# A fused attention and two-MLP kernel: the second product of the first MLP through DRAM by a seven-product scheme, the attention on fixed half steps

## The chip, the cores and the metric

The kernel runs on one core of one Trainium2 chip. The metric is the device time of one execution in microseconds (us), the median over several executions; lower is better.

## What is computed

Three pieces follow each other, all in float32, on 8 batches of 576 tokens (4608 tokens in all, 512 features, 2048 hidden features):

```python
a = softmax(phi, axis=2)                     # (8, 8, 576, 32), exp after subtracting the maximum, sum + 1e-9
k_m = einsum('bhsm,bhsd->bhmd', a, k)        # memory of 32 rows per head
v_m = einsum('bhsm,bhsd->bhmd', a, v)
attn = softmax(q @ k_m.T / sqrt(64))
x = heads_to_features(attn @ v_m)            # (4608, 512)
x = (s * relu(x @ w_in1) ** 2 + b) @ w_out1  # first MLP, 512 -> 2048 -> 512
out = (relu(x @ w_in2) ** 2) @ w_out2        # second MLP, the same sizes
```

The weights arrive as 64-bit floats and are narrowed on the chip.

## The kernel before

All large matmuls take float32 operands as two rounded halves (fp32r), a high part (a cast on ScalarE) and a remainder (a subtraction on VectorE), and add three products of them; `split3` names the three. A matmul here is 128x128 weights against 256, 288 or 384 columns.

**Attention and first MLP, interleaved.** `attention(b)` (L219) is a generator that issues the attention of one batch in pieces: the softmax of phi, the memory products `kvs` (L272), their transposes (L317, L318), the transposes of q (L340), the scores (L355), their softmax, and the transposed probabilities `pt`, split in two (L392, L393). The values are not multiplied with the probabilities: `v_fold` (L469) multiplies them into w_in1 first (`vps`, L459) and splits the result in `vp`, so that the first product of the MLP, `h1` (L480), is `vp` times `pt`: six matmuls of 288 columns (half a batch) for each of the 16 blocks of 128 hidden features (L490). Its result is rectified, squared and split on ScalarE and VectorE (L496 to L499) into `g`, and `x1` (L502) at once multiplies `g` with the stored split w_out1: twelve matmuls of 288 columns (L507), accumulated over the 16 blocks in four PSUM banks. The sums leave through `x1_store` (L513) into DRAM (`x1d`). There are 256 such steps (8 batches, 2 halves, 16 blocks), in the order of the list `steps`, `h1` two steps ahead of `x1`. Between the matmul groups `slot()` counts places and `advance()` lets the attention of a later batch go on for a piece when its due place is reached; what a piece asks for in `yield` is how many places it wants to pass.

**Weights of the second MLP.** From step 66 on, `narrow` and `combine` (L109, L142) prepare the seven combinations of both weight matrices of the second MLP that a seven-product scheme (Strassen's, in Winograd's form) needs, and store them in DRAM (`wcd`, `wod`): 16 units, narrowed, summed and split on ScalarE and VectorE beside the steps.

**Second MLP.** It goes in two phases, each by the seven-product scheme. The first product (L803) goes over 6 pairs of 384-token halves; for each of eight units of hidden features and each of the seven products there are six matmuls of 384 columns. `sums` and `split_x` make the seven combinations of the input, `chain` adds the seven results into four quadrants, which are rectified, squared and stored in DRAM (`gd`). The second product (L868) reads them back in 18 blocks of 256 tokens, makes the seven combinations of each and runs 24 matmuls of 256 columns for each.

Pools: PSUM has 4 banks for `acc`, 2 for `hps` and 2 for everything else in the interleaved part, 8 free banks later. All loads and nearly all stores are issued by the SP queue, in program order. A scheduler orders each engine's instructions from the program; each engine then works through its own list in order.

## Time and profile before

| | |
|---|---|
| runs of the kernel (us) | 1501.75, 1505.45, 1505.59; median 1505.45 |
| the profiled execution | 1501.85 us, of which 1500.0 us from the first to the last instruction |
| TensorE (PE) busy | 1462.7 us (98%), weight loads (PEld) 1408.7 us |
| VectorE (DVE) busy | 930.8 us (62%) |
| ScalarE (ACT) busy | 800.0 us (53%) |
| GpSimd (POOL) busy | 1.0 us |
| DMA | 235.8 MB, 157 GB/s on the mean |
| mean granted TensorE clock | 0.994 of 2.4 GHz |

How to read it: an engine's busy time is the time in which at least one of its instructions was in work. TensorE's matmuls overlap each other, so that the mean duration of one is no measure of how many fit into a microsecond; the starts of equal groups are. The stages by TensorE: until 31.5 us the first batch's attention, until 777.6 us attention and first MLP interleaved, from 779.4 us the first product of the second MLP, from about 1134 us its second product. What lies outside of the span is 1.85 us in the profiled execution.

### The profile page before, as it was taken

Reading aid. Unit: us, or ns where it says so; the run is one execution under the profiler, and the core shown is the slowest. Engines: PE = TensorE matmul, PEld = TensorE weight load, DVE = VectorE, ACT = ScalarE, POOL = GpSimd, SP = SyncE. Lnnn points to the kernel's source line nnn. Section 1 sums busy time; section 2 is a strip of 40 time slices with the busy share of each in tenths; the row PEclk is TensorE's granted clock in tenths of the full one; section 3 lists DMA queues with packets and bytes.
Section 4 is the critical chain, followed back from the end, with each engine's and each line's share of the span. In section 5 each row is a group of like instructions: output and inputs, shape, how many; then the busy total and the mean of one; then the engine's idle time right before and its main releaser. Section 6 shows DMA issues by size and latency. Waiting matters only on the chain.

```text
span 1500.0 us, 29921 instructions
## 1 busy us (share of the span) xinstructions
PE 1462.7 (98%) x12400; PEld 1408.7 (94%) x12400; DVE 930.8 (62%) x1528; ACT 800.0 (53%) x1637; POOL 1.0 (0%) x7
## 2 busy tenths in 40 slices
PE   5899999999999999999999999999999999999998
PEld 4789989989989899998999999999999999999998
DVE  6985464866758667544234655656556776667774
ACT  4677565776757767656542543434344444444442
POOL 0000000000000000000000000000000000000000
PEclk8999999999999999999999999999999999999999
DMA  9763323537365363403218524435498444443431
GB/s 306 232 195 129 125 80 96 168 128 238 122 240 175 132 230 129 164 28 134 81 50 346 169 97 157 151 103 183 162 331 321 141 138 132 139 132 122 138 116 29
DMA packets 157559, 235.77 MB, mean 157 GB/s; under 512 B 44912, under 2 KB 130928, under 8 KB 148848
## 3 DMA queue, kind: packets, MB, share of 16 engines
q1 hardware_dynamic: 157264, 233.60, 46.7%
q8 instruction: 97, 1.59, 0.4%
q14 instruction: 38, 0.31, 0.1%
q10 hardware_dynamic: 160, 0.26, 0.0%
HBM read 145.49 MB, written 88.34 MB: 156 GB/s over the span
## 4 chain that ended last, share of the span: by engine, by line
PE 88%; DVE 5%; DMA 5%; ACT 2%; issue 1%; SPq 0%; ACTq 0%; DVEq 0%
PE acc L507 24%; PE qa L868 13%; PE pa L803 13%; PE hps L490 12%; PE qc L868 7%; PE pc L803 6%; PE qb L868 3%; PE pb L803 3%; PE vps L459 2%; DMA kv<-in_v_dram 2%; DMA gd<-gr 1%; PE sp L355 1%; PE qps L340 1%; PE kvs L272 1%; DMA wt<-in_moe_w_in_dram 1%
## 5 line engine op out<-in xcount | busy, mean ns | idle before, releaser
L507 PE MATMUL acc<-g,wo 128*128 128x288 f32 (+1 forms) x3072 | 468.5, 299 | 0.4 <-DVE wo L138 0.3
L507 PEld LDWEIGHTS acc<-g,wo 128*128 128x128 f32 x3072 | 425.0, 189 | 23.2 <-ACT r L497 11.7
L490 PE MATMUL hps<-pt,vp 128*128 128x288 f32 x1536 | 257.2, 301 | 1.7 <-DVE pt L393 0.9
L499 DVE TENSOR_TENSOR g<-r,g 128x288 fp32r<-128x288 f32 x256 | 116.4, 456 | 196.3 <-ACT g L498 193.8
L490 PEld LDWEIGHTS hps<-pt,vp 128*128 128x128 f32 x1536 | 220.9, 190 | 12.5 <-issue 7.5
L868 PE MATMUL qa<-w,gc 128*128 128x256 f32 x1728 | 216.2, 283 | 1.3 <-ACT o L731 1.1
L803 PE MATMUL pa<-xc,w 128*128 128x384 f32 x1152 | 213.4, 337 | 1.5 <-issue 1.4
L868 PEld LDWEIGHTS qa<-w,gc 128*128 128x128 f32 x1728 | 210.7, 191 | 1.7 <-ACT o L731 1.3
L803 PEld LDWEIGHTS pa<-xc,w 128*128 128x128 f32 x1152 | 202.1, 188 | 2.1 <-issue 1.6
L496 ACT ACTIVATE r<-hps 128x288 f32<-128x288 f32 x256 | 105.1, 411 | 164.9 <-PE hps L490 162.0
L756 DVE TENSOR_TENSOR gc<-h,gc 128x1024 fp32r<-128x1024 f32 x102 | 124.6, 1223 | 92.8 <-ACT gc L755 92.8
L755 ACT CAST gc<-h 128x1024 fp32r<-128x1024 f32 x102 | 107.4, 1053 | 54.7 <-PE qb L868 27.2
L497 ACT ACTIVATE r<-r 128x288 f32<-128x288 f32 x256 | 113.6, 445 | 6.4
L498 ACT CAST g<-r 128x288 fp32r<-128x288 f32 x256 | 110.5, 432 | 6.2
L868 PE MATMUL qc<-w,gc 128*128 128x256 f32 x864 | 109.3, 283 | 0.4 <-ACT gc L755 0.4
L803 PE MATMUL pc<-xc,w 128*128 128x384 f32 x576 | 108.5, 337 | 0.0
L868 PEld LDWEIGHTS qc<-w,gc 128*128 128x128 f32 x864 | 105.9, 191 | 0.7 <-ACT gc L755 0.7
L803 PEld LDWEIGHTS pc<-xc,w 128*128 128x128 f32 x576 | 101.2, 188 | 0.0
L811 DVE SCALAR_TENSOR_TENSOR gr<-gr 128x384 f32<-128x384 f32 x144 | 79.5, 557 | 3.7
L720 DVE TENSOR_TENSOR gr<-pa,gr 128x384 f32<-128x384 f32 x48 | 26.5, 554 | 66.7 <-PE pa L803 66.7
L720 DVE TENSOR_TENSOR gr<-pb,gr 128x384 f32<-128x384 f32 x48 | 26.6, 554 | 66.4 <-PE pb L803 43.3
L808 ACT ACTIVATE gr<-pa 128x384 f32<-128x384 f32 x48 | 23.6, 491 | 72.1 <-PE pa L803 72.0
(261 smaller groups left out, 1440.0 us busy)
## 6 DMA issues: line engine op xcount, KB each, us to landing
gd<-gr SPq DMA_DIRECT2D x96, 384.0 KB, 3.5
h<-gd SPq DMA_DIRECT2D x34, 1024.0 KB, 4.8
wt<-in_moe_w_out_dram SPq DMA_DIRECT2D x16, 1024.0 KB, 5.3
q<-in_q_dram SPq DMA_DIRECT2D x72, 128.0 KB, 3.1
x1d<-xo SPq DMA_DIRECT2D x16, 576.0 KB, 3.6
out_dram<-o SPq DMA_DIRECT2D x70, 128.0 KB, 2.3
kv<-in_k_dram SPq DMA_DIRECT2D x23, 384.0 KB, 5.0
kv<-in_v_dram SPq DMA_DIRECT2D x23, 384.0 KB, 6.4
```

What stands on the lines that cost most here:

```text
L490: nc.tensor.matmul(hps[:, :NB1], lhsT=w[:, wi], rhs=pt[xi][:, hp, t0:t0 + NB1], start=(i == 0), stop=(i == 5))
L496: nc.scalar.activation(r[:, :NB1], hps[:, :NB1], AF.Relu)
L497: nc.scalar.activation(r[:, :NB1], r[:, :NB1], AF.Square)
L498: st["act"] = nc.scalar.copy(g[0][:, :NB1], r[:, :NB1])
L499: st["dve"] = nc.vector.tensor_tensor(out=g[1][:, :NB1], in0=r[:, :NB1], in1=g[0][:, :NB1], op=ALU.subtract)
L507: nc.tensor.matmul(acc[d][:, :n], lhsT=wo1[:, f, wi, d * P:d * P + P], rhs=g[xi][:, :n], start=(first and i == 0), stop=(store is not None ...
L720: nc.vector.tensor_tensor(out=out, in0=bank, in1=other, op=ALU.add)
L755: nc.scalar.copy(c[:, :, 0, :], of)
L756: nc.vector.tensor_tensor(out=c[:, :, 1, :], in0=of, in1=c[:, :, 0, :], op=ALU.subtract)
L803: nc.tensor.matmul(to, lhsT=w[:, wi, k], rhs=xc[e][:, xi, k], start=(start and n == 0), stop=(n == 5), skip_group_check=True)
L811: nc.vector.scalar_tensor_tensor(out=done, in0=done, scalar=0.0, in1=done, op0=ALU.max, op1=ALU.mult)
L868: nc.tensor.matmul(to, lhsT=casts[n, e][:, u, xi], rhs=w[:, wi].rearrange("p k c -> p (k c)"), start=(start and u == 0 and i == 0), stop=( ...
```

## The change

The first MLP is taken apart in two phases like the second.

**Phase one, attention and first product.** The list of steps, `x1` and the paced generators are gone. There are 256 half steps (`slot`), each one call of `hidden`: the same six matmuls as in `h1`, then only the rectification, on ScalarE, into a tile `r` (128 x 576). Each pair of half steps stores `r` to DRAM (`rd`). The pieces of the attention of later batches are laid over the half steps by a table, `on(slot, piece)`: in each batch of 32 half steps the scores, memory products and folds of a later batch stand at places 8, 16 and 24, the q transposes at 4, 13 and 21, and so on. All of batch 1's softmax of phi and memory products stand ahead of the first half step. PSUM has 3 banks for `hps`, 2 for `kvs` and 3 for everything else. In the second to fourth batch `wo1_narrow` narrows w_out1, and GpSimd adds up its rows (`wacc`, eight operations of 128x1024) for the bias term; in the last two batches `wo1_combos` makes the seven combinations of w_out1 in SBUF.

**Phase two, second product by seven products.** Nine blocks of 512 tokens. `quad` loads the four quarters (128 x 2048 each) of a block from `rd`; ScalarE squares them, `sums` makes seven combinations in place, and each is cast and split in two halves (128 x 1024); 48 matmuls of 256 columns for each of the seven products. The combinations are asked for three half products ahead (`ready1.upto`); the pool `c` has five buffers for them. The results leave with scale and bias to `x1d`.

**Weights of the second MLP.** `combine` for w_in2 runs in phase two of the first MLP (one piece at each half product), for w_out2 in the first product of the second MLP. `chain` and `sums` take the seven products in another order everywhere, and `sums` needs no extra tile; the second MLP's loops are the same otherwise. All of its first weights are loaded at the end of phase two, into the tiles that w_out1's combinations held.

```diff
     ND = DM // P
     NV = DFF // 512
-    NB1 = S // 2
+    HB = S // 2
+    NU = NF // 2
     TP = 384
     NPAIR = NT // (2 * TP)
...
-    SEGS += [(b, half, 0, NF) for b in range(2, B) for half in range(2)]
-    SLOTS = 6
+    TB = 512
+    NBLK1 = NT // TB
+    NBLK2 = NT // 256
+    XG = 1536
+    SB = 2 * NF
...
+    rd = [[dram.tile([P, NU, S], F32, name=f"rd{b}_{h}") for h in range(2)] for b in range(B)]
...
+    def fold(b, n):
+        w = c_p.tile([P, 2, 2, 512], F32R, tag="c", name="vp")
+        ts = [bank("vps") for _ in range(2)]
...
+            nc.scalar.copy(w[:, hp, 0, :], t)
+            nc.vector.tensor_tensor(out=w[:, hp, 1, :], in0=t, in1=w[:, hp, 0, :], op=ALU.subtract)
+        at["vp", b, n] = w
...
+    def hidden(b, f, half, r):
+        pt = at["pt", b]
         hps = ps_h.tile([P, 512], F32, tag="h", name="hps")
...
+        t0 = half * HB
...
-            w = folded[b, f // 4][:, hp, :, (f % 4) * P:(f % 4) * P + P]
-            for wi, xi in ((0, 0), (0, 1), (1, 0)):
-                nc.tensor.matmul(hps[:, :NB1], lhsT=w[:, wi], rhs=pt[xi][:, hp, t0:t0 + NB1],
+            w = at["vp", b, f // 4][:, hp, :, (f % 4) * P:(f % 4) * P + P]
+            for wi, xi in split3:
+                nc.tensor.matmul(hps[:, :HB], lhsT=w[:, wi], rhs=pt[xi][:, hp, t0:t0 + HB],
                                  start=(i == 0), stop=(i == 5))
                 i += 1
-            slot()
-        r = tmp.tile([P, NB1], F32, tag="r", name="r")
-        g = g1[at % 3]
-        nc.scalar.activation(r[:, :NB1], hps[:, :NB1], AF.Relu)
-        nc.scalar.activation(r[:, :NB1], r[:, :NB1], AF.Square)
-        st["act"] = nc.scalar.copy(g[0][:, :NB1], r[:, :NB1])
-        st["dve"] = nc.vector.tensor_tensor(out=g[1][:, :NB1], in0=r[:, :NB1], in1=g[0][:, :NB1], op=ALU.subtract)
-        return g
-
-    def x1(acc, b, half, f, g, first, store):
-
-        n = NB1 + 2 if (b, half) == (0, 0) else NB1
+        nc.scalar.activation(r[:, t0:t0 + HB], hps[:, :HB], AF.Relu)
+
...
+    def wo1_narrow(u):
+
+
...
+            two = rc_p.tile([P, 2, 2, 512], F32, tag="rc", name="wo1")
+            wo1[u], wo1[u + 1] = two[:, 0], two[:, 1]
+        yield from narrow(t, wo1[u])
+        yield
+        if u == 0:
+            nc.gpsimd.tensor_copy(wacc, wo1[u])
+        else:
+            nc.gpsimd.tensor_tensor(out=wacc, in0=wacc, in1=wo1[u], op=ALU.add)
+
...
-    def x1_store(acc, b, half, part, last, keep):
-
-
-        t0 = b * S + half * NB1
...
-            if not last:
-                if part is None:
-                    nc.scalar.copy(o[:, d], src)
-            elif d % 2:
-                nc.vector.tensor_scalar(out=o[:, d], in0=src, scalar1=s_sb[:, 0:1], scalar2=wsum[:, d:d + 1],
-                                        op0=ALU.mult, op1=ALU.add)
-            else:
-                nc.scalar.activation(o[:, d], src, AF.Identity, scale=s_sb[:, 0:1], bias=wsum[:, d:d + 1])
-            if d == ND - 1 and not keep:
-                nc.sync.dma_start(x1d[t0 // XG][:, :, t0 % XG:t0 % XG + NB1] if last else partd[b][half], o)
-        store.o = o
-        return store
-
...
+    def wo1_combos(u):
+        tiles = unit_tiles(u)
+        for i, t in enumerate(tiles):
+            w2["one", u, i] = t.bitcast(F32R)
+        yield from combos(of_out(wo1.pop(u)), lambda: w2["one", u, 0], lambda: w2["one", u, 1])
...
+    def quad(n, h, j):
+        t = rc_p.tile([P, NU, 256], F32, tag="rc", name=f"r{h}{j}")
+        t0, t1 = n * TB + j * 256, n * TB + j * 256 + 256
         a = t0
...
+            m = min(t1 - a, S - a % S)
+            nc.sync.dma_start(t[:, :, a - t0:a - t0 + m], rd[a // S][h][:, :, a % S:a % S + m])
+            a += m
+        return t
...
+    def block_ready(n):
+        def cast(e, of):
+            for uh in range(2):
+                c = c_p.tile([P, NU // 2, 2, 256], F32R, tag="c", name="rcast")
+                src = of[:, uh * NU // 2:(uh + 1) * NU // 2]
+                nc.scalar.copy(c[:, :, 0, :], src)
+                nc.vector.tensor_tensor(out=c[:, :, 1, :], in0=src, in1=c[:, :, 0, :], op=ALU.subtract)
+                cast1[n, e, uh] = c
+        b11, b12, b22, b21 = quads.pop(n)
+        return sums(b11, b12, b21, b22, cast, lambda t: nc.scalar.activation(t, t, AF.Square))
...
+    front(0)
+    w1_narrow(0)
+    for g in range(NJG):
+        kvs(0, g)
+    kv_norm(0)
+    front(1)
+    kv_turn(0)
...
+    events = {}
+
+    def on(slot, go, *args):
+        events.setdefault(slot, []).append(lambda: go(*args))
+
+    for n in range(1, NV):
+        on((6, 14, 22)[n - 1], fold, 0, n)
+    for i in range(4, 2 * NV):
+        on((8, 10, 16, 18)[i - 4], w1_narrow, i)
+    for b in range(1, B):
+        z = SB * (b - 1)
+        for g, a in enumerate((8, 16, 24)):
+            on(z + a, scores, b, g)
...
+            y = SB * (b - 2) + (8 if b == 2 else 0)
+            for g, a in enumerate((8, 16, 24)):
+                on(y + a, kvs, b, g)
+            on(y + 26, kv_norm, b)
...
+        for n in range(NV):
+            on(z + 8 * n + 8, fold, b, n)
+        for g, a in enumerate((4, 13, 21)):
+            on(z + a, q_turn, b, g)
+        for g, a in enumerate((9, 17, 25)):
+            on(z + a, q_exp, b, g)
+            on(z + a + 1, q_sum, b, g)
+        for g, a in enumerate((13, 21, 29)):
+            on(z + a, p_turn, b, g)
+    on(SB * 5 + 21, wo1_sum)
+
...
+    for slot in range(SB * B):
...
+        if half == 0:
+            r = r_p.tile([P, S], F32, tag="r", name="r")
+        hidden(b, f, half, r)
+        if half == 1:
+            nc.sync.dma_start(rd[b][f // NU][:, f % NU], r)
...
+    def chain(e, banks, n, run, name):
+
+
+        key = "acacaba"[e]
+        start = e in (0, 1, 5)
+        if start:
+            banks[key] = bank(name + key)
+        to = banks[key][:, :n]
+        run(to, start)
+        return to
...
-    def advance():
-
-        task, pace = tasks[0]
...
-    def slot():
-        work["at"] += 1
-        if tasks and work["at"] >= work["due"]:
-            advance()
...
+    for n in range(NBLK1):
+        banks, outs = {}, {}
+        if n == NBLK1 - 1:
+            for _ in win:
+                pass
+            w64x.close()
...
+        for e in range(7):
+
+            def run(to, start):
+                for uh in range(2):
+                    half = 14 * n + 2 * e + uh + 3
+                    ready1.upto(half // 14, half % 14 // 2)
+                    next(win, None)
+                    for d in range(2):
+                        for u in range(NU // 2):
+                            w = weight("one", uh * NU // 2 + u, e)
+                            for i, (wi, xi) in enumerate(split3):
+                                nc.tensor.matmul(
+                                    to[:, d * 256:d * 256 + 256], lhsT=w[:, wi, d], rhs=cast1[n, e, uh][:, u, xi],
+                                    start=(start and uh == 0 and d == 0 and u == 0 and i == 0),
+                                    stop=(uh == 1 and u == NU // 2 - 1 and i == 2), skip_group_check=True)
+            to = chain(e, banks, 512, run, "y")
+            which, high = ((0, 0), (1, 1), (0, 1), (0, 1), (1, 1), (0, 0), (1, 0))[e]
+            key = which, high
+            if key not in outs:
+                outs[key] = o1_p.tile([P, 2, 256], F32, tag="o", name="yo")
+                for d in range(2):
+                    nc.scalar.activation(outs[key][:, d], to[:, d * 256:d * 256 + 256], AF.Identity,
+                                         scale=s_sb[:, 0:1], bias=wsum[:, 2 * which + d:2 * which + d + 1])
+            else:
+                o = outs[key].rearrange("p d t -> p (d t)")
+                nc.vector.scalar_tensor_tensor(out=o, in0=to, scalar=s_sb[:, 0:1], in1=o, op0=ALU.mult, op1=ALU.add)
+            if e > 2:
+                t0 = n * TB + high * 256
+                nc.sync.dma_start(x1d[t0 // XG][:, 2 * which:2 * which + 2, t0 % XG:t0 % XG + 256], outs[key])
+            if e == 4 and n + 1 < NBLK1:
+                quads[n + 1] = [quad(n + 1, *hj) for hj in QUADS]
```

What this does to the order of the engines' lists shows at three places.

VectorE ahead of the first half step. Before, from the first batch's row sums to the first split probabilities (`rs` are the row sums, `kb` the turned keys, `m_` and `l_` maxima and sums of the scores, `vp` the folded weights, `pt` the probabilities):

```order
L303 RECIPROCAL rs<-rs 128x2
L130 TENSOR_SCALAR wx<-wx 128x1024
L131 SCALAR_TENSOR_TENSOR wx<-wt,wx 128x1024
L324 COPY kb<-kvt 64x4x32
L133 SCALAR_TENSOR_TENSOR w_0_157<-wt,wx 128x1024
L324 COPY kb<-kvt 64x4x32
L367 TENSOR_REDUCE m__399<-sp 128x12
```

and now, from the same row sums (`pm` are maxima of phi, `ph` phi, `es` its sums):

```order
L328 RECIPROCAL rs<-rs 128x2
L93 TENSOR_SCALAR wx<-wx 128x1024
L95 SCALAR_TENSOR_TENSOR wx<-wt,wx 128x1024
L99 SCALAR_TENSOR_TENSOR w_0_165<-wt,wx 128x1024
L270 TENSOR_REDUCE pm<-ph 128x128
...
L289 TENSOR_TENSOR ph<-ph,t_343 128x4x96 x3
...
L297 TENSOR_REDUCE es<-ph 128x128
L347 COPY kb_169<-kvt 64x4x32 x2
...
L270 TENSOR_REDUCE pm<-ph 128x128
L415 TENSOR_TENSOR vp<-vps,vp 128x512
L372 TENSOR_REDUCE m__441<-sp 128x12
```

The second batch's softmax of phi, and a maximum of the third's, now stand between the first batch's row sums and its scores.

ScalarE in the middle of the interleaved part, before (rectify, square and cast of three steps):

```order
L496 ACTIVATE r<-hps 128x288
L497 ACTIVATE r<-r 128x288
L498 CAST g_2_173<-r 128x288
L496 ACTIVATE r<-hps 128x288
L497 ACTIVATE r<-r 128x288
L498 CAST g_0_169<-r 128x288
```

and now, eight half steps (`qT` are turned queries, `pt` probabilities, `x` scores):

```order
L378 ACTIVATE x<-x 128x384
L414 CAST vp<-vps 128x512 x2
L429 ACTIVATE r<-hps 128x288 x5
L357 COPY qT<-qps 128x384 x2
L399 CAST pt_2861<-pp 128x192 x2
L429 ACTIVATE r<-hps 128x288 x3
```

One operation stands for each half step where three stood, and the attention's operations stand in bursts between them.

VectorE in phase two, from the last combination of one block into the next (`r_5742` is the first block's quarter b21, `r_6179`, `r_6182` and `r_6184` are b11, b12 and b22 of the block after it; `yo` the results, `wx` a weight that is narrowed); before, there is no such place:

```order
L176 TENSOR_TENSOR r_5742<-r_5742,r_5735 128x2048
L495 TENSOR_TENSOR rcast<-r_5742,rcast 128x4x256 x2
L700 SCALAR_TENSOR_TENSOR yo<-ya,s_sb,yo 128x512
L495 TENSOR_TENSOR rcast<-r_6179,rcast 128x4x256 x2
L700 SCALAR_TENSOR_TENSOR yo<-yb,s_sb,yo 128x512
L176 TENSOR_TENSOR r_6179<-r_6182,r_6179 128x2048
L176 TENSOR_TENSOR r_6182<-r_6184,r_6182 128x2048
L495 TENSOR_TENSOR rcast<-r_6179,rcast 128x4x256 x2
L93 TENSOR_SCALAR wx<-wx 128x1024
L176 TENSOR_TENSOR r_6179<-r_6184,r_6179 128x2048
L95 SCALAR_TENSOR_TENSOR wx<-wt,wx 128x1024
L495 TENSOR_TENSOR rcast<-r_6179,rcast 128x4x256 x2
```

On ScalarE the square of b22 stands between the two casts of the next block's first combination:

```order
L494 CAST rcast<-r_5742 128x4x256 x2
L494 CAST rcast<-r_6179 128x4x256
L498 ACTIVATE r_6184<-r_6184 128x2048
L494 CAST rcast<-r_6179 128x4x256
L498 ACTIVATE r_6186<-r_6186 128x2048
L494 CAST rcast<-r_6179 128x4x256 x2
```

and on the SP queue the load of b22 (here `r_7075`) stands behind two stores of w_in2's combinations (`wid`) and a store of results:

```order
L483 DMA r_7073<-rd_0_93 128x8x256
L149 DMA wid_72<-wc 128x2048
L151 DMA wid_72<-wc 128x1536
L703 DMA x1d_67<-yo 128x2x256
L483 DMA r_7075<-rd_1_94 128x8x256
```

The tile of b22 of the next block is the one that b11 of the block held until the first row of VectorE's list above.

## Rows read from the trace of the kernel before

**Rows 1.** The page: busy time of the engines; TensorE in 40 slices, tenths.

```profile
PE 1462.7 (98%) x12400; PEld 1408.7 (94%) x12400; DVE 930.8 (62%) x1528; ACT 800.0 (53%) x1637; POOL 1.0 (0%) x7
...
PE   5899999999999999999999999999999999999998
```

**Rows 2.** Stages: stretch, length, busy (x instructions) PE, PEld, DVE, ACT, POOL; clock, DMA.

```profile
0.00:31.50 31.50, 14.99 (x269) 10.84 (x269) 21.00 (x37) 13.54 (x31) 0.95 (x7) 0.92 0.91 305
31.50:777.60 746.10, 732.55 (x7091) 684.09 (x7090) 461.27 (x899) 492.89 (x1134) 0.00 (x0) 0.99 0.44 145
```

**Rows 3.** Timeline of PE at 715 us: start, duration, instructions.

```profile
714.71 0.95 PE L490 MATMUL hps<-pt,vp 128*128 128x288 f32 x6
715.51 1.75 PE L507 MATMUL acc<-g,wo 128*128 128x288 f32 x12
717.10 0.95 PE L490 MATMUL hps<-pt,vp 128*128 128x288 f32 x6
```

**Rows 4.** The chain of waits in order of time, in the second MLP: start, duration.

```profile
916.29 2.12 PE pa L803 x12
...
1157.79 2.87 PE qb L868 x24
```

**Rows 5.** Costliest groups, TensorE: count, busy us, mean ns of one, idle before.

```profile
L507 PE MATMUL acc<-g,wo 128*128 128x288 f32 (+1 forms) x3072 | 468.5, 299 | 0.4 <-DVE wo L138 0.3
```

**Rows 6.** Groups of TensorE in the attention.

```profile
L459 PE MATMUL vps<-w,vmT 64*32 64x512 f32 x512 | 37.4, 601 | 0.0
...
L272 PE MATMUL kvs<-kv,e 64*32 64x128 f32 x1104 | 23.1, 287 | 11.9 <-DMA kv<-in_v_dram 9.3 <-ACT e L256 2.6
L355 PE MATMUL sp<-kb,qT 128*64 128x64 f32 x552 | 22.7, 231 | 1.1 <-DVE kb L324 1.1
L340 PE MATMUL qps<-ident,q 128*128 128x128 f32 x144 | 22.1, 282 | 0.9 <-ACT qT L346 0.6 <-ACT vmT L325 0.2
```

**Rows 7.** Groups of ScalarE and VectorE.

```profile
L756 DVE TENSOR_TENSOR gc<-h,gc 128x1024 fp32r<-128x1024 f32 x102 | 124.6, 1223 | 92.8 <-ACT gc L755 92.8
L499 DVE TENSOR_TENSOR g<-r,g 128x288 fp32r<-128x288 f32 x256 | 116.4, 456 | 196.3 <-ACT g L498 193.8 <-PE qps L340 1.9
L497 ACT ACTIVATE r<-r 128x288 f32<-128x288 f32 x256 | 113.6, 445 | 6.4
L498 ACT CAST g<-r 128x288 fp32r<-128x288 f32 x256 | 110.5, 432 | 6.2
...
L755 ACT CAST gc<-h 128x1024 fp32r<-128x1024 f32 x102 | 107.4, 1053 | 54.7 <-PE qb L868 27.2 <-PE qa L868 24.8 <-DMA h<-gd 2.7
...
L465 DVE TENSOR_TENSOR vp<-vps,vp 128x512 fp32r<-128x512 f32 x64 | 41.6, 686 | 13.0 <-ACT vp L464 12.5
L131 DVE SCALAR_TENSOR_TENSOR wx<-wt,wx 128x1024 int32<-128x1024 int32 x32 | 39.2, 1224 | 0.8
...
L130 DVE TENSOR_SCALAR wx<-wx 128x1024 int32<-128x1024 int32 x32 | 22.0, 692 | 14.0 <-ACT wx L129 13.5
...
L227 DVE TENSOR_REDUCE pm<-ph 128x128 f32<-128x1152 f32 x8 | 17.7, 2216 | 3.9 <-DMA ph<-in_phi_dram 3.8
...
L157 DVE TENSOR_TENSOR ws<-wx 128x256 f32<-128x256 f32 x32 | 12.0, 417 | 0.0
```

**Rows 8.** Stages again: a stretch of the start, a crowded stretch, the rest.

```profile
28.00:32.00 4.00, 3.41 (x23) 2.31 (x23) 3.75 (x9) 2.43 (x5) 0.00 (x0) 0.50 1.06 387
31.50:80.00 48.50, 43.15 (x563) 38.64 (x562) 43.01 (x71) 32.99 (x71) 0.00 (x0) 0.91 0.76 242
80.00:777.60 697.60, 689.41 (x6528) 645.44 (x6529) 418.27 (x829) 459.90 (x1063) 0.00 (x0) 1.00 0.41 138
```

**Rows 9.** DMA issues: out<-in, queue, count, KB each, median us to landing.

```profile
h<-gd SPq DMA_DIRECT2D x34, 1024.0 KB, 4.8
...
w<-wcd SPq DMA_DIRECT2D x8, 768.0 KB, 12.3
```

**Rows 10.** Stages again: one pair of the second MLP's first product.

```profile
837.60:896.60 59.00, 59.00 (x341) 59.00 (x340) 35.11 (x62) 25.19 (x49) 0.00 (x0) 1.00 0.41 134
```

More of the change, by code (lines that the diff above doesn't have):

```diff
@@ new lines, in combine, with get, go @@
+    def combine(load, quads_of, dst, raw_tile, second_tile):
+        t = raw_tile([P, 2, 512], I64, "wt")
+        load(t)
+        yield
+        x = yield from narrow(t, None)
+        yield
+        made = {}
+        def get(key, tile, shape):
+            def go():
+                if key not in made:
+                    made[key] = tile(shape, F32R, "wc")
+                return made[key]
+            return go
+        first, second = get(0, raw_tile, [P, 4, 2, 2, P]), get(1, second_tile, [P, 3, 2, 2, P])
+        for w in combos(quads_of(x), first, second):
+            if w == "second":
+                nc.sync.dma_start(dst[:, 0:4], made[0].bitcast(F32))
+            yield
+        nc.sync.dma_start(dst[:, 4:7], made[1].bitcast(F32))
@@ L757, in cast @@
             casts[n, e] = c
-        return sums(*raws.pop(n), (NU, P), cast)
+        return sums(*raws.pop(n), cast)
     def raw_first():
```

937 lines of the change are left out of this document (399 added, 538 removed).

## The prediction

> **What bounds the kernel now.** The page comes first: TensorE is busy 98% of the span and in every slice after the first two [rows 1], so time is saved only where TensorE gets less to do, and lost where it is made to wait. The stages come second: until 31.5 us it works 15.0 us, then 732.6 of 746.1 us in the interleaved part [rows 2]; from 779.4 us on (the first matmul of its first product) the second MLP takes the remaining 720.6 of the span's 1500.0 us. The starts of equal groups come third, because the mean of one matmul is no price: one step of 6 and 12 matmuls of 288 columns starts 2.39 us after the one before [rows 3], 0.1328 us for a matmul. In the second MLP 12 matmuls of 384 columns take 2.12 us and 24 of 256 columns 2.87 us [rows 4], 0.1196 us for one of 256.
>
> So the 256 steps are 611.8 us of the interleaved part. TensorE's other 120.7 busy microseconds there and its 15.0 ahead of it are the attention: 135.7 us.
>
> **What the change removes and adds, in order of time.** w_out1's product goes from 3072 matmuls of 288 columns [rows 5], 408 us, to 9 blocks x 7 products x 48 matmuls of 256, 3024 of them, 361.6 us: 46 us less if TensorE alone decides. The 1536 matmuls of the first product stay, 204.0 us, and so does the attention.
>
> *Start.* The first half step stands at 31.5 us [rows 2]. Now the second batch's softmax of phi, the third's maxima and a third group of scores stand ahead of it on VectorE: two maxima and a sum over a phi tile at about 2.2 us [rows 7], three subtractions and small pieces, some 12 us in all, and about 2 us for what TensorE and ScalarE do in between. Phi of the second batch is the last of the first 6.8 MB of loads; at the 305 GB/s of the start [rows 2] it lands at 22 us, about when VectorE asks for it. I take 46 us; 40 if half of it overlaps, 55 if the loads come late.
>
> *Attention beside half steps.* Of the 135.7 us, some 17 lie ahead of the first half step: two batches of memory products (a quarter of 23.1), one of q transposes and one of scores (an eighth of 22.1 and of 22.7), one fold in 32 (1.2) [rows 6], and about 4 of smaller ones. There remain 118.7, with the half steps 322.7 us.
>
> *Stalls in this phase.* ScalarE had 506 us to do until 777.6 [rows 2]; squares and casts leave it (113.6 and 110.5 [rows 7]), which leaves at most 282. VectorE loses the 116.4 of L499 and, with the second MLP's weights, 16 combinations of about 7.4 each (0.69 + 2 x 1.22 + 8 x 0.42 + 0.95 [rows 7]); against its 482 that leaves about 250, and 34 come for w_out1's combinations (8 times 8 x 0.42 + 0.95, the same pieces). So TensorE stays the fullest of the three, but in a phase of half the length. Two rows bound what the waits cost: the calm stretch has 8.2 us of idle time on 689.4 [rows 8], 1.2% or 4 us here; the crowded one has 48.5 us for 43.15 busy and a mean clock of 0.91 [rows 8], 1.235 times what it needs, or 76 us here. VectorE is as full in the first batch after the start as in that stretch (some 45 us); the others lie near the calm one. I take 0.235 x 45 + 0.035 x 278 = 20 us, 3.5% being an estimate between the calm 1.2% and the crowded rate. The clock belongs to this: after idle TensorE time at the start, it was granted 0.50 of 2.4 GHz, the 1.2 GHz level, from 28 to 32 us [rows 8], so that a stop costs more than its own length. Stores of `r` (37.7 MB) take the place of the 46 MB of the second MLP's weights, which move to later stages; the phase needs about 90 MB in 390 us, 231 GB/s, and 305 were seen. They hide, unless a burst delays the four `r` buffers; that is in the 76.
>
> *Change of phase.* The first casts stand on ScalarE before the last half steps; 1.5 us for a last combination, 0 to 5.
>
> *Phase two.* One block needs 7 x 48 matmuls, 40.2 us. ScalarE does 14 casts at 1.05 and 4 squares of 2048 at about 1.9, well below. VectorE does 14 remainders of 1024 (17.1), 4 subtractions of 2048 (9.2, at 2.30 each, by the step from 0.417 for 256 to 1.223 for 1024), 3 results of 512 from PSUM at about 0.69 (2.1) and one weight combination (7.4) [rows 7]: 35.8 us. That would hide, but the lists tie a loop. From the end of the last subtraction in a block: the load of b22 into the freed tile, its square 1.93, the held-back cast 1.05, remainder 1.22, a result 0.69, two subtractions 4.6; then VectorE's own rest until the same place, 10 remainders 12.2, two subtractions 4.6, a result 0.69 and the weight's 7.4. That is 34.4 us and the load. A load of 1 MB lands 4.8 us after its issue [rows 9]; here two stores of 1.8 MB are in the queue ahead of it, 6 us at 305 GB/s, most of which has drained by then. I take 7.0: the loop is 41.4 us, above TensorE's 40.2, and nine blocks are 372.6. With 4.8 the blocks are 361.6; with 12.3, the landing of the loads that pile up when the second MLP's weights come [rows 9], 46.7 a block and 420.
>
> *Into the second MLP.* All 14.7 MB of its first weights are issued when the last block's fourth product ends; the first 8.4 MB take 27 us at 305 GB/s, of which 17 lie under the three products left, and the second part of unit 0 is wanted 8.5 us after the phase begins. I take 5 us of waiting, between 1 and 12. The combinations of w_out2 add 10 us of VectorE to each pair of the first product, which takes 59.0 us and has 35.1 of VectorE [rows 10]: the idle 24 hide them, and a pair would be late only if these were gone. w_in2's are in the sum of phase two. The new order of products and the sums in place I cost at nothing: VectorE's 11 operations of 1.22 and four casts of 1.05 in their chain are 17.6 us, below the 20.1 of 7 x 2.87.
>
> **The sum.** 46 + 322.7 + 20 + 1.5 + 372.6 + 5 = 767.8 us until the second MLP, against 779.4; with 720.6 behind it 1488.4. The profiled execution had 1.85 us outside its span, so 1490.2 against its 1501.85: 11.6 us less. The median shown is 3.6 above that execution; I predict 1492, and take changes against 1505.45, where 0.3% (4.5 us) is about what a measurement of this kernel can tell from no change.
>
> **A page against this change.** The eight GpSimd additions in the second to fourth batch have no row here: POOL's 1.0 us is all at the start [rows 1, 2]. The Trainium skill, page SBUF — State Buffer, section Who interferes with whom, says that a VectorE instruction with two SBUF inputs and a GpSimd instruction that reads SBUF exclude each other for a whole instruction. By that rule VectorE would stand still for each of them, which is the fourth rival; no run here shows it yet.
>
> **Rivals.**
> 1. *All of the gain comes.* The loads land at 4.8, the waits are the calm 4 us, the second MLP's weights cost 2: 46 + 322.7 + 4 + 1 + 361.6 + 2 + 720.6 + 1.85 = 1460. For it: VectorE's 35.8 is below 40.2, and TensorE was never stopped long after 100 us. Against it: the loop above has no slack at all. Chance 0.18.
> 2. *Half steps starve TensorE (slower).* A half step is 0.80 us, and three `hps` banks are 2.4 us of slack; each burst of ScalarE (two folds, two copies, two casts in a row) or a late VectorE stops it and takes the clock down. At the crowded rate the phase loses 76 instead of 20 us: 1548. It decides from 33 us of stalls on. For it: DVE, ACT and DMA were all full in just that stretch. Against it: after the start, before, the same attention went by with 1.2%; it had three times the TensorE work beside it. Chance 0.22.
> 3. *Phase two hangs on its loads (slower).* At 12.3 us a load the loop is 46.7 and the time 1540; it decides from 8.4 us on (1.45 us a block). For it: the stores in front. Against it: nothing else is as long in the queue as at the weights' loads. Chance 0.12.
> 4. *GpSimd holds VectorE.* A VectorE addition of this shape is 1.22 us [rows 7]; eight times that, all reaching TensorE, is 10 us: 1502, no change. For it, only the page; against it, a batch has about 9 us of VectorE to spare there. Chance 0.03.
>
> **How the numbers follow.** The forecast has 0.45, its own range 1478 to 1508: of that 0.34 lies more than 0.3% below 1505.45, 0.09 within, 0.02 above. Rival 1 is faster. Of rival 2, 0.02 is within and 0.20 slower, of rival 3, 0.02 and 0.10; rival 4 is within. So faster 0.52, same 0.16, slower 0.32. The range for 8 in 10 goes from 1460, all of the gain, to 1532, inside the two slow rivals: half of rival 1 and about half of the slow ones lie outside.
>
> **What would show it.** Right: the first half step near 46 us, phase two's first matmul near 390 and blocks 41 us apart, VectorE nearly without idle time in them and ScalarE waiting for a load ahead of the square of b22; the first matmul of the second MLP near 768, and 720 us after it. Wrong in the stalls: the last half step past 425 us, with TensorE waiting for `r` or `vp` and slices of a lower clock. Wrong in the loop: blocks 40.2 or 45 apart. Wrong at the root: blocks whose 24 matmuls are not 2.87 us apart, or a second MLP that is longer than 720 us, since I gave it no new wait.

## The result

The changed kernel takes 1482.67 us (median of 4 runs, 1475.95 to 1484.82) against 1504.88 us before (4 runs; the prediction had three of them, median 1505.45): 0.9849 of it, with a 95% interval of 0.9812 to 0.9886, so it is 1.1 to 1.9% faster. The prediction was 1492 us and faster by 0.9%. The profiled execution, 1484.73 us with a span of 1482.9, stands at the upper end of its runs.

The profile after, first the engines, TensorE's slices and its clock on the page:

```profile
PE 1418.3 (96%) x12240; PEld 1365.3 (92%) x12240; DVE 1055.7 (71%) x1461; ACT 793.8 (54%) x1371; POOL 19.4 (1%) x16
...
PE   3899899989999999999999999999999999999998
...
PEclk9999999999999999999999999999999999999999
```

TensorE has 44.4 us less to do than before [rows 1], 160 records of matmuls fewer; but four slices of the first nine are below 9 now, where before only the first two were. The stages, by the start of each one's first matmul (columns as in [rows 2]):

```profile
0.00:52.80 52.80, 22.95 (x439) 15.61 (x439) 32.73 (x52) 15.87 (x33) 1.21 (x8) 0.97 0.97 300
52.80:385.60 332.80, 315.47 (x3737) 275.39 (x3737) 226.50 (x429) 218.59 (x536) 18.23 (x8) 0.98 0.70 229
385.60:757.20 371.60, 361.76 (x3025) 358.88 (x3026) 289.65 (x282) 237.60 (x273) 0.00 (x0) 1.00 0.62 202
757.20:1110.20 353.00, 351.82 (x2019) 350.09 (x2018) 255.33 (x450) 171.19 (x331) 0.00 (x0) 1.00 0.70 252
1110.20:1482.90 372.70, 366.26 (x3025) 365.36 (x3023) 251.50 (x250) 150.58 (x199) 0.00 (x0) 0.99 0.41 135
```

The second MLP starts at 757.2 us instead of 779.4: 22.2 us are won there, and 5.1 of them are given back in it (725.7 us against 720.6). The forecasts for these stretches were 46, 344.2, 372.6 and, for the last two together with the wait into the second MLP, 725.6 us.

### The profile page after: what moved, and what is told of

Same layout as the page of the kernel before. It is cut to its first block, busy times and chain, and to the rows that moved or that the text cites. A ratio compares the mean times of both kernels' runs of the same rounds, so it can differ in the third digit from the quotient of the medians.

```text
span 1482.9 us, 29501 instructions
## 1 busy us (share of the span) xinstructions
PE 1418.3 (96%) x12240; PEld 1365.3 (92%) x12240; DVE 1055.7 (71%) x1461; ACT 793.8 (54%) x1371; POOL 19.4 (1%) x16
## 4 chain that ended last, share of the span: by engine, by line
PE 55%; DVE 8%; DMA 6%; ACT 3%; issue 2%; SPq 0%; ACTq 0%; DVEq 0%
PE qa L837 14%; PE pa L781 13%; PE qc L837 7%; PE pc L781 6%; PE ya L686 5%; DVE rcast L495 4%; DMA r<-rd 4%; PE qb L837 3%; PE pb L781 3%; PE yc L686 2%; DVE r L176 2%; ACT rcast L494 1%; DMA wt<-in_moe_w_in_dram 1%; DMA w<-wod 1%; PE yb L686 1%
## 5 line engine op out<-in xcount | busy, mean ns | idle before, releaser
L426 PE MATMUL hps<-pt,vp 128*128 128x288 f32 x1536 | 228.5, 303 | 12.1 <-ACT r L429 11.3
L686 PE MATMUL ya<-rcast,w 128*128 128x256 f32 x1728 | 210.2, 282 | 7.7 <-ACT yo L696 7.2
L686 PEld LDWEIGHTS ya<-rcast,w 128*128 128x128 f32 x1728 | 206.3, 188 | 9.9 <-ACT yo L696 9.0
L730 DVE TENSOR_TENSOR gc<-h,gc 128x1024 fp32r<-128x1024 f32 x119 | 145.2, 1224 | 97.0 <-ACT gc L729 97.0
L495 DVE TENSOR_TENSOR rcast<-r,rcast 128x1024 fp32r<-128x1024 f32 x126 | 150.5, 1219 | 74.8 <-ACT rcast L494 74.7
L494 ACT CAST rcast<-r 128x1024 fp32r<-128x1024 f32 x126 | 127.7, 1048 | 35.3 <-DVE r L176 33.3
L498 ACT ACTIVATE r<-r 128x2048 f32<-128x2048 f32 x36 | 69.1, 1919 | 77.7 <-DMA r<-rd 77.7
L686 PE MATMUL yc<-rcast,w 128*128 128x256 f32 x864 | 106.2, 281 | 2.6 <-DVE rcast L495 1.9
L686 PEld LDWEIGHTS yc<-rcast,w 128*128 128x128 f32 x864 | 103.7, 188 | 3.5 <-DVE rcast L495 2.5
L176 DVE TENSOR_TENSOR r<-r,r 128x2048 f32<-128x2048 f32 x36 | 82.3, 2287 | 0.7
```

The lines of the kernel that those rows point to most:

```text
L176: less = lambda out, in0, in1: lambda: nc.vector.tensor_tensor(out=out, in0=in0, in1=in1, op=ALU.subtract)
L426: nc.tensor.matmul(hps[:, :HB], lhsT=w[:, wi], rhs=pt[xi][:, hp, t0:t0 + HB], start=(i == 0), stop=(i == 5))
L494: nc.scalar.copy(c[:, :, 0, :], src)
L495: nc.vector.tensor_tensor(out=c[:, :, 1, :], in0=src, in1=c[:, :, 0, :], op=ALU.subtract)
L498: return sums(b11, b12, b21, b22, cast, lambda t: nc.scalar.activation(t, t, AF.Square))
L686: nc.tensor.matmul(to[:, d * 256:d * 256 + 256], lhsT=w[:, wi, d], rhs=cast1[n, e, uh][:, u, xi], start=(start and uh == 0 and d == 0 and ...
```

## The experiments

Times of a kernel are compared with the kernel before on the same chip. In the kernels below that leave attention and half steps as they are in the changed kernel, phase two began between 379.3 and 386.3 us (385.6 in the changed kernel), and in those that leave phase two alone it took 369.0 to 372.0 us (371.6 in the changed kernel): differences inside these bounds are not read as effects. Runs for which no interval is given were executed once.

### The start: the second batch's phi later

In the changed kernel TensorE waits 13.09 us for VectorE's maximum of that phi. VectorE in this time waits 5.45 us for ScalarE, narrows a weight, waits 1.67 us more for phi, whose load was issued at 21.70 us, and starts on it at 26.14. The first half step follows at 52.8 us (timelines of VectorE and PE):

```profile
26.14 2.09 DVE L270 TENSOR_REDUCE pm<-ph 128x128 f32<-128x1152 f32 x1 [1.67 <-DMA ph<-in_phi_dram]
28.28 0.48 PE L276 MATMUL t<-ident,pm 128*128 128x128 f32 x1 [13.09 <-DVE pm L270]
...
52.83 1.48 PE L426 MATMUL hps<-pt,vp 128*128 128x288 f32 x4 [0.41 <-ACT pt L399]
```

```diff
     kv_norm(0)
-    front(1)
     kv_turn(0)
...
         p_turn(0, g)
+    front(1)
     for g in range(NJG):
         kvs(1, g)
```

> The second batch's softmax of phi is issued behind the first batch's probabilities instead of ahead of its turned keys. Theory A (the start is long because TensorE and VectorE, each working in order, stand 13.1 us at the second batch's phi, whose load is issued at 21.7 us and lands at 26.1): the first half step comes at 36 to 40 us instead of 52.8, TensorE's idle time until 80 us falls from 32 us to about 20, and the whole is 8 to 13 us shorter than 1482.7, near 1472. Rival B (the loads set the start: the DMA share is near 1 from 20 to 55 us and again from 75 to 120, so that the half steps that come earlier only wait later): the first half step is early too, but the last half step still starts within 3 us of 385, and the whole stays within 3 us of 1482.7.

Measured: 1489.02 us, 0.9913 of before (0.9896 to 0.9930). The stages:

```profile
0.00:46.40 46.40, 23.28 (x278) 13.31 (x278) 26.13 (x43) 13.47 (x26) 1.21 (x8) 1.00 0.91 282
46.40:388.00 341.60, 318.85 (x3900) 277.18 (x3900) 232.69 (x439) 219.91 (x543) 17.75 (x8) 1.00 0.70 231
```

The first half step comes 6.4 us earlier and the last one 2.3 us later: the wait is real, but ending it is worth nothing here, and theory A falls. Rival B holds for the last half step; the whole, 6.3 us above the changed kernel's, is outside its 3 us, and why is not known. TensorE's idle time (stretch less busy) goes from 29.9 to 23.1 us ahead of the first half step and from 17.3 to 22.8 behind it. The next batch's keys show one possible reason: with the memory products later their buffers come free later, and SP issues these loads at 54.53 instead of 40.72 us. Whether the loads or VectorE (busy for 28.2 of the first 33.6 us of half steps) hold the half steps then was not separated.

### Phase two: what holds a block

Groups of 48 matmuls of 256 columns start 5.68 us apart when nothing waits, so a block needs 7 x 5.68 = 39.76 us. The starts of the sixth product (`yb`) of the changed kernel are 40.32, 44.22, 42.18, 41.25, 40.26, 42.56, 40.24 and 40.65 us apart. TensorE waits mostly for the copy of a product's result (L696), in six of these nine waits the first product's; only in the longest interval, 44.22, do casts cost it more, 2.6 us against 1.1 (waits of PE, 385.6 to 757.2 us):

```profile
PE ya L686 <- ACT yo L696: 7.2, 9, 1.7
PE yc L686 <- DVE rcast L495: 1.9, 1, 1.9
```

Timeline of the fourth block, PE and then ScalarE:

```profile
515.97 6.07 PE L686 MATMUL yc<-rcast,w 128*128 128x256 f32 x48
523.73 5.95 PE L686 MATMUL ya<-rcast,w 128*128 128x256 f32 x48 [1.69 <-ACT yo L696]
```

```profile
505.68 1.92 ACT L498 ACTIVATE r<-r 128x2048 f32<-128x2048 f32 x1 [2.43 <-DMA r<-rd]
507.50 1.03 ACT L494 CAST rcast<-r 128x1024 fp32r<-128x1024 f32 x1
512.05 1.92 ACT L498 ACTIVATE r<-r 128x2048 f32<-128x2048 f32 x1 [3.52 <-DMA r<-rd]
513.87 1.98 ACT L494 CAST rcast<-r 128x1024 fp32r<-128x1024 f32 x2
515.75 1.02 ACT L696 ACTIVATE yo<-ya,wsum,s_sb 128x256 f32<-128x256 f32 x2
...
520.76 2.00 ACT L494 CAST rcast<-r 128x1024 fp32r<-128x1024 f32 x2 [2.96 <-DVE r L176]
522.66 1.01 ACT L696 ACTIVATE yo<-ya,wsum,s_sb 128x256 f32<-128x256 f32 x2
```

The square at 512.05 is that of b21, which the sixth product needs at 540.9 us. It waits 3.52 us for its load, and behind it stand the casts of the second combination, the casts of the third (held by VectorE, which is late for the same reason), and the result copy that TensorE wants. VectorE is busy 289.65 of 371.6 us, so it has 9.1 us a block to spare; 70.5 us of its waits there are for ScalarE's casts. Four runs asked what ends this.

**Without the weights' combinations.** `for u in range(NU)` in `win` becomes `range(1)`, and `wid` is one tile.

> The combinations of w_in2 are made for one unit instead of eight in phase two; the other seven units' load, narrowing, sums, splits and stores are left out and all units read the first one's tile. Changed kernel: blocks about 41.3 us apart, 371.6 in all, TensorE waiting 0.8 us a block for the result copy of the first product. Theory A (the predicted loop: the load of b22 and then VectorE's own work, 7.4 us a block of it for the weights): the loop falls by 7.4 us, TensorE alone decides, blocks 40.3 us apart, phase two 363 to 365, VectorE idle below 4 us a block. Rival B (the load is late because stores and weight loads share its queue): also 40.3, with the load landing in 5 us instead of 7.0. Rival C (the casts cannot run far enough ahead because five buffers hold the split combinations and TensorE frees them): the stall stays above 0.5 us a block although VectorE has 7.4 us less to do.

Measured: 1477.65 us, phase two 365.6; the full quarters of 1 MB land in 5.9 us at the median (7.0 in the changed kernel).

```profile
383.50:749.10 365.60, 361.12 (x3025) 358.74 (x3026) 246.96 (x198) 215.37 (x231) 0.00 (x0) 1.00 0.47 150
```

Phase two is 6.0 us shorter, so a part of the stall goes. Five of eight intervals are 39.9 to 40.3, the rest up to 42.4: a stall stays, although VectorE has 42.7 us less to do and idles 13 us a block, where theory A looked for under 4. The edit takes away VectorE's work, 22 us of ScalarE's and seven units' loads and stores together, so it does not say which of them the 6.0 us belong to.

**With the combinations, without the stores of seven of the eight units.**

> The combinations of w_in2 are all computed, but the stores of seven of eight units (1.8 MB a block) are left out and all units read the first one's tile. Theory A (VectorE's work in the loop): its 7.4 us a block stay, blocks about 41.0 to 41.3 apart. Rival B (the stores delay the load of b22 in the queue): the load lands in 5 to 5.5 us instead of 7.0, and blocks are 40.3 to 40.5 apart. Rival C (buffers): the load lands earlier and a part of the stall goes, 40.5 to 41.0.

Measured: 1476.47 us, phase two 369.8, inside the bounds, with the quarters landing in 6.1 us. The stores are not what holds the blocks; rival B falls.

**A sixth buffer for the split combinations.** Here and in the next run three buffers for results instead of five make room.

```diff
+                count[0] += 1
+                pool = more[0] if more and count[0] % 6 == 0 else c_p
-                    half = 14 * n + 2 * e + uh + 3
+                    half = 14 * n + 2 * e + uh + 4
```

> One more buffer for the split combinations in phase two, and they are asked for four half products ahead instead of three (result buffers 3 instead of 5 to make room). Theory A (VectorE's own work and the load fill the loop): nothing to gain, blocks stay 41.3 us apart. Rival C (the casts cannot run ahead because five buffers are freed by TensorE): one half product, 2.9 us, more slack, blocks 40.3 apart, phase two 363 to 365, and 7 to 9 us less in all, near 1475. Against both: with three result buffers a result may wait for its store, which would show as TensorE waiting for a result copy at the second product.

Measured: 1480.35 us, 0.9849 (0.9833 to 0.9866), as the changed kernel; phase two 368.2 and not 363 to 365, five intervals still above 40.9. Rival C falls.

**A buffer of its own for b22.**

```diff
+        own = r2 and (h, j) == (1, 1) and n < NBLK1 - 1
-        t = rc_p.tile([P, NU, 256], F32, tag="rc", name=f"r{h}{j}")
+        t = (r2[0] if own else rc_p).tile([P, NU, 256], F32, tag="rc", name=f"r{h}{j}")
```

> In phase two b22 of the next block gets a buffer of its own (result buffers 3 instead of 5 make room), so that its load starts when b22 of the block has been cast, some 14 us earlier, and b11, b12 and b21 share four buffers. Theory D (the loop runs over the loads because each of the four quarters can only be loaded into a tile that the block just before gives back; the chain of waits goes through these loads block after block): blocks 39.8 to 40.3 us apart, phase two 360 to 364 instead of 371.6, ScalarE's waits for loads below 30 us instead of 71.9, the whole 8 to 11 us less than 1482.7, near 1473. Rival A (VectorE's own work fills the loop): blocks stay at 41.3. Rival C (the five buffers of split combinations): the gain stays at or below the 3.4 us of phase two that a sixth one brought.

Measured: 1484.74 us, 0.9889 (0.9871 to 0.9907); phase two 372.8. ScalarE waits as long for loads as in the changed kernel (waits of ScalarE, 390 to 750 us; first the changed kernel, then this run):

```profile
ACT r L498 <- DMA r<-rd: 71.9, 30, 6.6
```

```profile
ACT r L501 <- DMA r<-rd: 68.6, 28, 5.4
```

Theory D falls in this form: the load of b22 starts earlier, but the scheduler then puts the squares elsewhere, again ahead of where their loads have landed, and copies wait behind them.

**The order of ScalarE's list.** An edge of order, without a wait, puts each square behind the last result copy traced ahead of it:

```diff
+            ins = nc.scalar.activation(t, t, AF.Square)
+            if yos:
+                tc.add_manual_dep(ins.ins, yos[-1].ins.name, mybir.DependencyInfo(
+                    mybir.DependencyClass.NoSync, mybir.DependencyReason.DATA), reason="square")
```

> Phase two of the changed kernel with one rule more for ScalarE's list: a square may not be issued ahead of the last result copy that stands before it in the program (an order on ScalarE's own list, no wait for another engine). So b22 is squared behind the sixth product's result, and b21 behind the third's, instead of both ahead of the second combination's casts. Theory E (the loads land in time for their own use, but the squares stand too early in ScalarE's list, wait there for their loads, b21's four products before it is used, and hold the casts and result copies behind them): ScalarE's waits for loads fall from 71.9 us to below 40, TensorE's waits in phase two from 10.3 to 0 to 4 us, blocks 39.8 to 40.6 us apart, phase two 360 to 365 instead of 371.6, the whole 6 to 11 us less than the changed kernel. Theory D (the loads themselves are late): blocks still 41 or more apart, phase two above 368.

> The same rule together with the buffer of its own for b22 (result buffers 3 instead of 5). Theory E: no more than 2 us beyond the run with the rule alone. Theory D: this run alone falls to 360 to 365 us in phase two. Both needed: the rule alone 365 to 368, this one 360 to 363.

Measured: the rule alone 1477.10 us, 0.9834 (0.9819 to 0.9848), phase two 369.2; with b22's buffer 1473.49 us, 0.9800 (0.9782 to 0.9818), phase two 366.6. The two stages:

```profile
379.30:748.50 369.20, 363.07 (x3024) 360.35 (x3025) 288.54 (x281) 240.06 (x274) 0.00 (x0) 1.00 0.62 203
```

```profile
385.40:752.00 366.60, 362.21 (x3024) 361.05 (x3025) 289.25 (x281) 238.79 (x274) 0.00 (x0) 0.99 0.62 205
```

By its total, and by phase two, the rule alone cannot be told from the changed kernel. Inside phase two it can: ScalarE's waits for quarters fall to 26.5 and 26.2 us as theory E wants, and the middle answers. With the rule alone the third to seventh intervals are 39.76 to 40.74, below the 41.4 of the predicted loop, although b22's tile and VectorE's work are as in the changed kernel; with both the second to fourth are 39.76 to 39.77. But the first is 43.8 and 45.5, the last of the rule alone 43.3, and TensorE still waits 6.0 us with the rule alone, so both expectations in us were missed. In the second block another operation of ScalarE does what the squares did (timeline of ScalarE in the run with both):

```profile
429.37 1.14 ACT L91 ACTIVATE wx<-wt 128x1024 f32<-128x1024 f32 x1 [3.50 <-DMA wt<-in_moe_w_in_dram]
430.42 1.01 ACT L707 ACTIVATE yo<-ya,wsum,s_sb 128x256 f32<-128x256 f32 x2
431.31 1.91 ACT L502 ACTIVATE r<-r 128x2048 f32<-128x2048 f32 x1
```

The scaling of w_in2's piece waits for its load with the result copy behind it. So the same edge went to that operation:

> The run with the rule and b22's own buffer, and the same rule for the first operation on w_in2's pieces in phase two (the scaling on ScalarE that waits for the weights' load): it may not be issued ahead of the last result copy that stands before it in the program either. In the run before, ScalarE stood 3.5 us at that load in the second block, with the sixth product's result behind it, and TensorE waited 2.6 us at 439 us. Theory E: that wait goes, phase two falls from 366.6 to 361 to 364 us, no interval between blocks above 43 us, the whole 1468 to 1474. Theory D: a load that stands in the way is only replaced by another; phase two stays within 1.5 us of 366.6.

Measured: **1468.18 us**, 0.9764 of before (0.9749 to 0.9779). The stage, and its sixth products:

```profile
381.90:740.80 358.90, 358.43 (x3025) 358.06 (x3026) 288.49 (x281) 238.45 (x274) 0.00 (x0) 1.00 0.64 209
```

```profile
530.62 5.84 PE L700 MATMUL yb<-rcast,w 128*128 128x256 f32 x48
536.30 11.52 PE L700 MATMUL ya<-rcast,w 128*128 128x256 f32 x96
```

Seven of eight intervals are 39.76 us and one 40.34; phase two is TensorE's own time. It is 7.7 us shorter than in the run before, which lacks only the last edge, and 12.7 shorter than in the changed kernel. VectorE is busy as long as there (288.5 us) and ScalarE too (238.5): no work was taken away, and theory E stands. This version is faster than both kernels. The 12.7 us belong to the two rules and b22's own buffer together; whether the rules need the buffer was not tried.

### The half steps: four looks at ScalarE and GpSimd

**The first block's squares on GpSimd.**

```diff
+            if n == 0 and (t is b11 or t is b12):
+                nc.gpsimd.tensor_tensor(out=t, in0=t, in1=t, op=ALU.mult)
```

> The squares of the first block's b11 and b12 go from ScalarE to GpSimd. In the changed kernel ScalarE stands 2.0 and 2.7 us at 322 and 328 us before them, waiting for their loads, with rectifications of half steps behind them. Theory: TensorE's waits of 0.7 and 2.4 us at 325 and 331 us go, and the lower granted clock of 0.91 from 320 to 340 us behind them, so that the phase of half steps ends 4 to 6 us earlier (phase two begins at 380 to 382 instead of 385.6); the whole 3 to 6 us less. Rival (the time is given back at the change of phase, where the first block's casts are late in any case): phase two begins within 1.5 us of 385.6.

Measured: 1484.38 us, 0.9865 (0.9847 to 0.9883); phase two begins at 384.8, inside the bounds. From 300 us on half steps wait 7.5 us for ScalarE (6.9 in the changed kernel). The rival holds: the time is only waited elsewhere.

**Two banks for the half steps.** `ps_h` 2 buffers, `ps_m` 4.

> Two PSUM banks instead of three for the half steps, four instead of three for the rest of the attention. Forecast's rival (bursts of ScalarE starve TensorE; a bank is 0.8 us of slack): waits of half steps for ScalarE rise from 11.3 us by 15 to 40 us, the first matmul of phase two comes at 400 to 425 us. If instead ScalarE's waits were only the few long ones (2.7, 2.4, 1.3 us) and the rest well inside the slack, the rise is 5 to 10 us, with phase two at 391 to 396.

Measured: 1499.48 us, phase two from 403.2 us. Waits for ScalarE double (waits of PE, 50 to 780 us; the changed kernel has 11.3 in 11):

```profile
PE hps L426 <- ACT r L429: 23.5, 24, 4.1
```

17.6 us later, with 12.2 us more of this wait: between the two expectations in the wait, in the first one's range in the time. Rival 2's mechanism is there; three banks leave 11.3 us of it.

**GpSimd's additions.** The changed kernel, timelines of GpSimd, VectorE and TensorE:

```profile
177.97 2.38 POOL L462 TENSOR_TENSOR wacc<-wacc,wo 128x1024 f32<-128x1024 f32 x1 [8.81 <-DVE wo L99]
```

```profile
178.01 2.42 DVE L280 COPY mxb<-mx 128x128 f32<-128x128 f32 x1
```

```profile
185.60 0.66 PE L426 MATMUL hps<-pt,vp 128*128 128x288 f32 x3 [2.74 <-ACT r L429]
```

The copy ends 0.08 us after the addition. From 180 to 200 us the granted clock's mean is 0.91:

```profile
180.00:200.00 20.00, 17.26 (x156) 15.99 (x139) 13.64 (x27) 11.81 (x32) 0.34 (x1) 0.91 0.54 172
```

```diff
         if u == 0:
             nc.gpsimd.tensor_copy(wacc, wo1[u])
-        else:
-            nc.gpsimd.tensor_tensor(out=wacc, in0=wacc, in1=wo1[u], op=ALU.add)
```

> The seven additions on GpSimd are left out (the bias term then holds the first eighth of w_out1's sums only); the lists of ScalarE and VectorE are the same otherwise. Forecast's fourth rival (GpSimd holds VectorE): the broadcast copy at 178.0 us takes 0.2 instead of 2.42 us, TensorE's wait of 2.7 us at 182.9 goes, the granted clock of 180 to 200 us is 1.00 instead of 0.91, and phase two begins 3 to 5 us earlier, at 380.5 to 382.5. Rival (that copy is late by chance, or the wait for ScalarE has another cause): a copy above 1 us, or a wait at the same place of over 1.5 us, remains, and phase two begins within 1.5 us of 385.6.

Measured: the copy takes 0.21 us, the wait falls to 0.61, the clock is 1.00, phase two begins at 380.5, and the whole, 1478.44 us, lies within the changed kernel's runs:

```profile
179.62 0.21 DVE L280 COPY mxb<-mx 128x128 f32<-128x128 f32 x1
```

```profile
185.09 1.19 PE L426 MATMUL hps<-pt,vp 128*128 128x288 f32 x7 [0.61 <-ACT r L429]
```

So GpSimd does reach TensorE: in eight of the other runs, all with the additions, the same wait is 2.71 to 2.74 us. Which operation of VectorE is held makes no difference to it. In six of these eight the copy takes 0.21 or 0.22 us, and the addition that follows on VectorE 2.60 instead of 0.41 (run with a sixth buffer):

```profile
179.66 0.22 DVE L280 COPY mxb<-mx 128x128 f32<-128x128 f32 x1
179.79 2.60 DVE L111 TENSOR_TENSOR ws<-wo 128x256 f32<-128x256 f32 x1
```

The clock does not follow the wait: from 180 to 200 us it is 1.00 in three of the eight too. Nor can the whole 5 us be put down to GpSimd: with the additions in place, phase two began at 379.3 us in the run with the squares' rule alone, and at 381.9 with all the rules.

**The copies on ScalarE** (`nc.scalar.copy` for `mxb`).

> The eight broadcast copies of the maxima of phi go from VectorE to ScalarE; GpSimd's additions stay. If the copy held by a GpSimd addition (2.42 instead of 0.23 us) is what cost the half steps 5 us in the changed kernel: phase two begins at 380 to 383 us, as without the additions (380.5), TensorE's wait of 2.7 us at 183 gone. If the additions hold VectorE's other operations as well: 384 to 386, with another operation of VectorE longer by over 1 us beside an addition.

Measured: 1481.82 us, phase two from 386.1. Here too that addition of VectorE is held (0.41 us otherwise):

```profile
178.23 2.57 POOL L462 TENSOR_TENSOR wacc<-wacc,wo 128x1024 f32<-128x1024 f32 x1 [5.96 <-DVE wo L99]
```

```profile
178.47 2.61 DVE L111 TENSOR_TENSOR ws<-wo 128x256 f32<-128x256 f32 x1
```

The wait of TensorE there is 0.34 us, and yet the stage is no shorter: until 380 us half steps wait 11.6 us for ScalarE in all (10.1 in the changed kernel, 6.9 without the additions), so other waits fill the place.

## Why the prediction was right

The sum was 1488.4 us of span and came out at 1482.9; the direction came from its main term, and that one is right. That the total is as close as 5.5 us is in part luck: the start took 6.8 us more than forecast and the half steps 11.4 less. Point by point:

- **TensorE's work.** 46 us less was forecast, 44.4 came off its busy time. The bound of phase two was a little high: 39.76 us a block, not 40.2, since 256 columns take 0.1183 us when nothing interferes.
- **The start**: 46 forecast, 52.8 measured. The mechanism, VectorE asking for the second batch's phi as it lands, was right. The landing was mis-sized: 22 us in the forecast, 26.1 in the trace, which is 4 of the 6.8 us; the rest was not followed. The first run shows that this term and the next are not independent: what the start gives back, the half steps take.
- **Stalls beside half steps**: 322.7 + 20 + 1.5 = 344.2 forecast, 332.8 measured. Most of the difference is no stall: TensorE was busy 315.5 us here and not 322.7, because 23.0 us of its work, not 17, lay ahead of the first half step. It idled 17.3 us where 21.5 were forecast, but not where they were: the crowded row [rows 8] gave 10.6 us for the first 45, where it idled 2.4 (52.8 to 98 us), and the rest got 9.7, where it idled 14.9. Rival 2 did not happen; with one bank less it would have come close (27.7 us idle; it decides from 33 on).
- **Phase two**: 372.6 forecast, 371.6 measured, and here the number is right for a wrong reason. The step that failed is "the lists tie a loop ... VectorE's own rest until the same place ... 34.4 us and the load". VectorE idles 9.1 us a block, where the prediction looked for nearly none; its other sign, ScalarE waiting for quarters, is there (71.9 us), and the landing (7.0 us median) was right. Taking the combinations, the stores or the buffers' limit away each left stalls; moving operations of ScalarE behind the result copies, with a buffer for b22, ended them with all the work in place. What holds a block is ScalarE's list: an operation that waits for a load stands in it ahead of a copy that could go.
- **Into the second MLP**: 5 us forecast, 1.0 measured: 0.36 and 0.68 us of waits, both for casts of the input and none for the weights that the term was about. The 5.1 us that the rest is longer were given no term. About 3 of them lie where its second product begins (timeline of PE, then the same place before the change):

```profile
1116.63 0.62 PE L837 MATMUL qa<-w,gc 128*128 128x256 f32 x3 [1.34 <-DMA w<-wod]
...
1118.65 0.80 PE L837 MATMUL qa<-w,gc 128*128 128x256 f32 x2 [1.05 <-ACT o L843]
1119.64 5.06 PE L837 MATMUL qa<-w,gc 128*128 128x256 f32 x22 [0.19 <-DVE gc L730]
1124.50 3.19 PE L837 MATMUL qc<-w,gc 128*128 128x256 f32 x24
```

```profile
1140.79 2.79 PE L868 MATMUL qa<-w,gc 128*128 128x256 f32 x22
1143.42 2.91 PE L868 MATMUL qc<-w,gc 128*128 128x256 f32 x23
```

```profile
1118.00:1125.00 7.00, 6.16 (x27) 5.87 (x28) 5.95 (x5) 4.08 (x7) 0.00 (x0) 0.51 1.04 399
```

  22 matmuls take 4.86 us instead of 2.63, at a granted clock of 0.51 (the 1.2 GHz level) after waits of 1.34, 1.05 and 0.19 us; before the change the waits here are 0.28, 1.06 and 0.45 us. In six of the twelve other runs these matmuls take 4.05 to 4.80 us, in six 2.72 to 2.74, and the rest takes 721.9 to 726.7 us: this part comes and goes.
- **Rival 4** had 0.03 and exists, but costs less than its 10 us: one of seven additions reached TensorE, for some 2 us (2.74 us of wait against 0.61). Beside the other six no operation of VectorE in the changed kernel is longer by more than about a quarter of a microsecond. The Trainium skill's rule on two inputs (page SBUF — State Buffer, section Who interferes with whom) agrees with the trace in VectorE's addition, which reads two tiles in SBUF: 0.41 us alone, 2.60 to 2.61 beside GpSimd's, to within 0.3 us of its end. The copy that was held in the changed kernel (2.42 us) has one input and is not a case of that rule. Operations of VectorE that read one input from PSUM kept their length beside an addition (L373 0.55, L415 0.64 us), as the section also has it.
- **Rivals 1 and 3** were two ends of the same stall: the last run reached 358.9 us in phase two, below rival 1's 361.6, with the order changed and a buffer for b22.

## What to carry to other kernels

In the list of an engine that works in order, no operation that waits for a load should stand in front of a result copy. Here edges of order at those few operations, with one buffer, took 12.7 us off a phase from which two extra buffers and two leavings-out, each by itself, had taken between nothing and 6; the last edge alone took 7.7. A load or an engine's work sum that fits the measured period is no proof that it sets it; look at what stands ahead of the waiting instruction in its own engine's list. And a start that is shortened is only worth something if what comes behind can take the work earlier: here 6.4 us bought nothing.

## What was not expected of the hardware

One addition on GpSimd made a copy of VectorE eleven times as long (0.21 to 2.42 us), and through it TensorE waited 2.74 us instead of 0.61, until 7.6 us after the addition began. Waits of 1.34, 1.05 and 0.19 us of TensorE with 1 us of work between them were followed by 22 matmuls at the 0.51 clock, but waits of 0.97, 1.05 and 0.48 at the same place in the run with two banks were not (22 matmuls in 2.74 us), nor were waits of 0.65, 1.94 and 1.07 us in phase two (mean clock 1.00 from 470 to 485 us); what decides it stays open. 1 MB in rows of 1 KB (`r` from `rd`) landed in 7.0 us at the median, and in 6.1 with most of the stores beside it left out.
